# Attention times V in two blocks per chunk instead of four, in a fused attention and gated MLP kernel

## The chip, the cores and the metric

The kernel runs on one core of one Trainium2 chip. The metric is the device time of one execution in microseconds (us); lower is better. Three runs of the kernel before took 557.98, 558.04 and 558.1 us, median 558.04.

## The reference

One layer norm feeds a sliding-window attention and a gated MLP; both results are added to the input.

```python
xn = _layernorm(x)                                # S = 2048 rows, D = 576
qkv = (xn @ wqkv)                                 # H = 32 heads of Dh = 18
scores = q @ k.T * Dh ** -0.5                     # key at most 255 rows back, none ahead
o = softmax(masked scores) @ v
A = o @ wo
B = (silu(xn @ w1) * (xn @ w3)) @ w2              # F = 4608
return x + A + B
```

Inputs and output are bfloat16.

## The kernel before, in words

**Recording.** The kernel is written as one list of operations in program order. A helper, `add`, gives each operation its engine, the buffers it reads (`r`), overwrites (`w`) or adds to (`j`), and derives the semaphore waits. Each engine then runs its own operations in that order: TensorE (PE), VectorE (DVE), ScalarE (ACT), GpSimd (POOL), and SyncE (SP), which only issues DMAs. ScalarE issues some DMAs too, in line with its computing. An operation that waits holds up everything behind it in its engine's queue.

**Chunks.** The 2048 rows are worked in four chunks of 512. In chunks 2 to 4 a chunk begins with the projections to q, k and v (`proj_part`, L490). Then come 36 *units*, then *phase 2*. In chunk 1 the projections are done ahead of the loop.

**Units.** A unit makes 128 of the 4608 hidden columns: 18 products of 64 rows by 128 columns by 512 (`unit_pairs`, L726), two at a time on the two halves of the array, nine into each of two PSUM banks. ScalarE computes a tanh of one bank (`unit_tanh`, L735), VectorE multiplies twice (`unit_h`, L741 and L744) and writes the hidden tile `hT[u]`. Six of the eight PSUM banks are three pairs, `JOBS`, which units and V blocks take in turn (`job()`); the other two, `SC`, are for the scores.

**Attention.** The 32 heads are 8 groups of four. A *score step* (`scores`, L610) makes a part of the scores of one group; ScalarE writes its exponentials into a slot (`exps`, L619), GpSimd masks them (`masks`, L646). There are 4 steps per group in chunk 1 and 5 in the others, 32 and 40 steps per chunk, dealt out between the products of the units by a hand-written clock that counts pairs of products. Slots for probabilities lie in a buffer of their own (`pt`, 10 slots), in the staging buffer of the projections (`sh`, 4 slots, chunks 2 to 4) and in tiles of `hT` that aren't computed yet (`h`, 4 slots in the last 8 tiles).

**V blocks.** When two groups (a pair) are done, `pv` (L667) multiplies their probabilities with V: 72 products in chunk 1 and 96 in the others, 64 rows by 20 columns, eight side by side, into one pair of banks. A column of ones in V gives the sums of the probabilities. Then VectorE copies each of the two banks out in transposed form (`pv_out`, L676), takes the reciprocal of the sums (L681), GpSimd scales (`o_scale`, L682) into one buffer `oq`, and VectorE turns the result back in two halves (`o_turn`, L689) into `od`. DMAs pack it into `oT` (`o_pack`, L714): four packs per pair, and eight small ones for the first pair, which ScalarE issues in chunk 1 and SP in the others. Three V blocks stand between units, the fourth after item 8 of phase 2.

**Phase 2.** `p2_item` (L797) multiplies `hT` with w2 and `oT` with wo, in products of 64 by 128 by 288, two at a time, and adds both into the same banks. Some 324 items; the first two read a part of `oT` that only the first pair fills; the other products with wo of the first half follow after 144 items with w2. VectorE adds the input and SP stores.

**Weights.** The weights of the units pass through three buffers `w13`, each for four units, in six loads of 192 KB on SP (`load_part`, L320). `owed` counts loads to be issued, one after every fifth product pair. Buffer 1 holds tiles of w2 during phase 2. In chunks 2 to 4 the loads for the next chunk's first four units are issued after the 28th unit, those for its second four units in phase 2. w2 is loaded in tiles of 288 KB, six tiles ahead (`load_w2`, L352), on ScalarE's queue during phase 2.

**What the change touches:** the slots (`pt_slot`, `pt_keys`), the two staging places for copies out (`uqs`), `exps`, `pv`, `o_scale`, and in the main loop `PV_COST`, `take`, `score_step`, the V block after a unit, the block in phase 2, and the weight loads after units and in phase 2.

Of the kernel before, what the change touches and what calls it, by code (L numbers as in the profile page):

```python
# [164 lines left out]
def bass_parallel_sum__sliding_block__glu_gated_swiglu__prompt_kernel(  # L165
# [32 lines left out]
    with ExitStack() as es:  # L198
# [5 lines left out]
        KB, NB, NV = 64, CH // 64, 12  # L204
        ident = sb("ident", [128, 128])
# [27 lines left out]
        def pt_slot(sl):  # L233
            kind, n = sl
            if kind == "pt":
                return pt[:, n, :, :]
            if kind == "sh":
                two = stage[:, 2 * n:2 * n + 2, :]
            else:
                two = hT[:, NF - 8 + 2 * n:NF - 6 + 2 * n, :]  # L240
            return two.rearrange("p t c -> p (t c)").rearrange("p (q r) -> p q r", r=2)

        def pt_keys(sl):
            kind, n = sl
            if kind == "pt":
                return [("pt", n)]
            if kind == "sh":
                return [("sh", 2 * n), ("sh", 2 * n + 1)]
            return [("h", NF - 8 + 2 * n), ("h", NF - 7 + 2 * n)]
# [5 lines left out]
        rden = sb("rden", [128, CH // 32], dt.float32)  # L255
# [292 lines left out]
        def span_issue(a, b, moves, first, only=slice(None)):  # L548
            seen = set()
            for n, (kind, eng, tset, dst, src) in enumerate(moves):  # L550
# [4 lines left out]
                add(eng, lambda e, dst=dst, src=src: e.dma_start(dst, src), r=st_keys(*tset), dma=f"{kind}_{a}",  # L555
# [59 lines left out]

        def exps(c, g, s, sl):
            pt_of[(c, g, s)] = sl
            w = KB * sum(nb for _, _, nb in steps_of(c)[s])
            add("act", lambda e: e.activation(  # L619
                pt_slot(sl)[:, 0:w, :], PS[:, SC[0]:SC[1] + 1, 0:w].rearrange("p r q -> p q r"), ACT.Exp, scale=scale),  # L620
                r=[("ps", b) for b in SC], w=pt_keys(sl))
# [27 lines left out]
        def pv(c, j, banks):  # L649
# [4 lines left out]
            for s, st in enumerate(steps_of(c)):  # L654
                col = 0
                for kb, q0, nb in st:
                    n += 1
                    pos = (c * NB + kb) % NV
                    for gi in range(2):
                        g = 2 * j + gi  # L660
                        sl = pt_of[(c, g, s)]
                        for pr in range(2):
                            for p in range(2):
# [8 lines left out]
                                    r=pt_keys(sl) + [("va", pos)], **{"j" if any(k[0] == p for k in seen - {(p, gi, pr)}) or not first else "w": [("ps", banks[p])]})  # L672
                    col += nb

        def pv_out(b, i):
            add("dve", lambda e: e.transpose(uqs[i], PS[:, b, :]), r=[("ps", b)], w=uq_keys[i])  # L676

        def o_scale(i):
            u3 = uqs[i].rearrange("p (n d) -> p n d", d=32)
            o3 = oq[:, :].rearrange("p (n d) -> p n d", d=32)[:, :, 0:Dh]  # L680
            add("dve", lambda e: e.reciprocal(rden[:], u3[:, :, Dh]), r=uq_keys[i], w=["rden"])  # L681
            add("pool", lambda e: e.tensor_tensor(  # L682
                o3, u3[:, :, 0:Dh], rden[:].unsqueeze(2).to_broadcast([128, CH // 32, Dh]), ALU.mult),
                r=uq_keys[i] + ["rden", "oq0"], w=["oq"])
# [306 lines left out]
        PV_COST, PV_AFTER = 6.6, 20  # L991
# [6 lines left out]
        for c in range(NC):  # L998
# [8 lines left out]
            total = 9 * NF + len(att) + 3 * PV_COST  # L1007
# [9 lines left out]
            if c:  # L1017
                free += [("sh", n) for n in range(4)]
            early = [("h", n) for n in range(4)]
# [7 lines left out]
            def take(n):  # L1027
                if n < len(early):
                    return early[n]
                return free.pop(0)  # L1030

            def score_step():
# [3 lines left out]
                sl = take(done)  # L1036
                exps(c, g, s, sl)
                masks(c, g, s)
                done += 1
                if done % (2 * NS) == 0:  # L1040
                    pv_ready[done // (2 * NS) - 1] = clock + PV_AFTER

            def spaced_step():
# [3 lines left out]
                room = last - clock - PV_COST * (3 - next_pv) - 5 * sum(v > at_u for v in xt)  # L1047
# [21 lines left out]
            for u in range(NF):  # L1069
# [16 lines left out]
                if u % 4 == 3 and u < NF - 8 and (c or u != 15):  # L1086
                    owed += 6
                if next_pv in pv_ready and clock >= pv_ready[next_pv] and next_pv < 3:
                    j = next_pv
                    next_pv += 1  # L1090
                    banks = job()
                    pv(c, j, banks)
                    clock += PV_COST
                    for g in (2 * j, 2 * j + 1):
                        for s in range(NS):
                            if pt_of[(c, g, s)][0] != "h":
                                free.append(pt_of[(c, g, s)])
                    later(u, lambda b=banks: (pv_out(b[0], 0), pv_out(b[1], 1), o_scale(0)))
                    later(u + 1, lambda j=j: (o_turn(2 * j, 0), o_turn(2 * j, 1), o_scale(1)))
                    later(u + 2, lambda j=j: o_turn(2 * j + 1, 0))  # L1100
                    later(u + 3, lambda j=j: o_turn(2 * j + 1, 1))
                    later(u + 5, lambda j=j: o_pack(j, "sp"))
                    if j == 0:
                        for n in range(4, 12, 1 if c == 0 else 2):
                            later(u + n + 1 if c == 0 else u + n // 2 + 4,
                                  lambda n=n: o_pack(0, "act", n, n + 1) if c == 0 else o_pack(0, "sp", n, n + 2))
# [33 lines left out]
            assert done == len(att) and next_pv == 3, (done, next_pv)  # L1140
# [9 lines left out]
            for item in p2_list(c):  # L1150
# [8 lines left out]
                elif n == 8:  # L1159
                    load_w2(c, AHEAD - 1, after=(last_pe(),))  # L1160
                    banks = jobs[NF - 2]
                    pv(c, 3, banks)
                    pv_out(banks[0], 0)
                    pv_out(banks[1], 1)
                    o_scale(0)
                    o_turn(6, 0)
                    o_turn(6, 1)
                    o_scale(1)
                    o_turn(7, 0)
                    o_turn(7, 1)  # L1170
                    o_pack(3, "sp")
# [7 lines left out]
                elif n in (170, 195, 220, 245, 270, 295) and c + 1 < NC:  # L1179
# [32 lines left out]
```

## Time and profile before

| | |
|---|---|
| median of three runs | 558.04 us |
| lowest and highest | 557.98 and 558.1 us |
| the profiled execution's span | 556.1 us |
| TensorE busy, granted clock | 99% of the span, full |
| products of units (L726), share of the chain that ended last | 51% |
| products of phase 2 (L797) | 29% |
| projections (L490) | 10% |
| scores (L610) | 6% |
| V blocks (L667) | 4% |
| VectorE, ScalarE, GpSimd busy | 56%, 46%, 29% |
| moved by DMA | 86 MB, mean 155 GB/s |

The profile is of one execution. The span runs from its first instruction to its last; the runs are timed around it and are 1.9 us longer. In a row of the timeline the first number is the start in us from the span's beginning, the second how long the row lasts, then the engine, the line, the operation, output and inputs, the shape and how many instructions were merged. In brackets stands how long the engine was idle before, and what ended it. Matmuls are pipelined: one lasts longer in a row than the time to the next one's start, so the distance of starts tells what a product costs.

### The profile page before, as it was taken

Reading aid. Unit: us, or ns where it says so; the run is one execution under the profiler, and the core shown is the slowest. Engines: PE = TensorE matmul, PEld = TensorE weight load, DVE = VectorE, ACT = ScalarE, POOL = GpSimd, SP = SyncE. Lnnn points to the kernel's source line nnn. Section 1 sums busy time; section 2 is a strip of 40 time slices with the busy share of each in tenths; the row PEclk is TensorE's granted clock in tenths of the full one; section 3 lists DMA queues with packets and bytes.
Section 4 is the critical chain, followed back from the end, with each engine's and each line's share of the span. In section 5 each row is a group of like instructions: output and inputs, shape, how many; then the busy total and the mean of one; then the engine's idle time right before and its main releaser. Section 6 shows DMA issues by size and latency. Waiting matters only on the chain.

```text
span 556.1 us, 18239 instructions
## 1 busy us (share of the span) xinstructions
PE 552.4 (99%) x8022; PEld 348.8 (63%) x8022; DVE 310.8 (56%) x587; ACT 257.6 (46%) x365; POOL 160.0 (29%) x380
## 2 busy tenths in 40 slices
PE   8999999999999999999999999999999999999998
PEld 4555445677687455477767645547777654555776
DVE  7466798610456778851056668884105567767211
ACT  7456776100286767600047776650005676666000
POOL 5323454300034445330003344533000333433000
PEclk9999999999999999999999999999999999999999
DMA  9997899677566556656856746566683684650650
GB/s 255 203 197 161 201 215 182 171 179 191 139 139 149 135 147 151 155 148 176 205 109 137 171 110 170 126 163 164 158 205 83 138 174 124 151 135 21 174 152 22
DMA packets 128038, 86.00 MB, mean 155 GB/s; under 512 B 35702, under 2 KB 125646, under 8 KB 127958
## 3 DMA queue, kind: packets, MB, share of 16 engines
q1 hardware_dynamic: 89138, 62.80, 49.7%
q10 hardware_dynamic: 38820, 22.02, 16.0%
q8 instruction: 63, 1.03, 0.8%
q14 instruction: 17, 0.14, 0.1%
HBM read 71.29 MB, written 2.36 MB: 132 GB/s over the span
## 4 chain that ended last, share of the span: by engine, by line
PE 98%; DMA 1%; ACT 0%; DVE 0%; issue 0%
PE ps L726 51%; PE ps L797 29%; PE ps L490 10%; PE ps L610 6%; PE ps L667 4%; DMA xp<-in_A_x_dram 1%; DVE stats L386 0%; ACT hT L380 0%; PE ps L419 0%; ACT sd L359 0%; ACT xnT L432 0%; DVE ofin L819 0%; DVE mv L389 0%
## 5 line engine op out<-in xcount | busy, mean ns | idle before, releaser
L726 PE MATMUL ps<-xnT,w 64*128 64x512 bf16 x1400 | 182.3, 376 | 0.0
L726 PE MATMUL ps<-xnS,w 64*128 64x512 bf16 x1120 | 155.3, 376 | 0.0
L797 PE MATMUL ps<-w,hT 64*128 64x288 bf16 x2292 | 143.9, 282 | 0.0
L741 DVE SCALAR_TENSOR_TENSOR gs<-th,ps 128x512 bf16<-128x512 bf16 x144 | 98.0, 681 | 80.1 <-ACT th L735 79.1
L619 ACT ACTIVATE pt<-ps 128x1024 bf16<-128x1024 f32 (+1 forms) x112 | 113.2, 1010 | 63.8 <-PE ps L610 62.5
L797 PEld LDWEIGHTS ps<-w,hT 64*128 64x128 bf16 x2292 | 112.0, 94 | 29.4 <-issue 0.4
L726 PEld LDWEIGHTS ps<-xnT,w 64*128 64x128 bf16 x1400 | 73.8, 94 | 55.0
L646 POOL TENSOR_TENSOR pt<-pt,mk 128x128 int32<-128x128 int32 (+1 forms) x199 | 80.3, 426 | 79.5 <-ACT pt L619 79.5
L744 DVE SCALAR_TENSOR_TENSOR hT<-gs,ps 128x512 bf16<-128x512 bf16 x144 | 98.9, 687 | 5.0
L735 ACT ACTIVATE th<-ps 128x512 bf16<-128x512 f32 x144 | 85.4, 593 | 22.2 <-PE ps L726 21.9
L726 PEld LDWEIGHTS ps<-xnS,w 64*128 64x128 bf16 x1120 | 60.1, 94 | 50.1
L503 ACT ACTIVATE stage<-ps 128x512 bf16<-128x512 f32 x16 | 9.6, 597 | 142.8 <-PE ps L490 140.5
L828 DVE TENSOR_TENSOR ofin<-ps,xp 128x288 bf16<-128x288 f32 x31 | 12.2, 451 | 110.3 <-PE ps L797 110.3
L646 POOL TENSOR_TENSOR hT<-hT,mk 128x128 int32<-128x128 int32 (+1 forms) x31 | 12.4, 420 | 170.5 <-ACT hT L619 170.5
L610 PE MATMUL ps<-qv,kv 64*128 64x320 bf16 (+4 forms) x528 | 53.8, 260 | 0.0
L610 PEld LDWEIGHTS ps<-qv,kv 64*128 64x128 bf16 x528 | 28.5, 94 | 24.7 <-issue 0.3
L490 PE MATMUL ps<-xnT,wp 64*128 64x512 bf16 (+1 forms) x360 | 39.0, 355 | 0.0
L619 ACT ACTIVATE stage<-ps 128x1024 bf16<-128x1024 f32 x24 | 24.6, 1024 | 12.6 <-PE ps L610 12.6
L689 DVE STREAM_TRANSPOSE od<-oq 128x256 bf16<-128x256 bf16 x64 | 25.8, 428 | 6.3 <-POOL oq L682 6.3
L490 PEld LDWEIGHTS ps<-xnT,wp 64*128 64x128 bf16 x360 | 20.6, 94 | 12.6 <-ACT va L539 0.4
L490 PE MATMUL ps<-wv,xnT 64*128 64x288 bf16 x288 | 22.1, 284 | 0.2 <-ACT xnT L432 0.2
L646 POOL TENSOR_TENSOR stage<-stage,mk 128x128 int32<-128x128 int32 (+1 forms) x42 | 16.9, 421 | 17.4 <-ACT stage L619 17.3
(73 smaller groups left out, 337.6 us busy)
## 6 DMA issues: line engine op xcount, KB each, us to landing
w<-in_B_w_dram SPq DMA_DIRECT2D x210, 192.0 KB, 4.3
w<-in_B_w_dram ACTq DMA_DIRECT2D x70, 288.0 KB, 3.5
xp<-in_A_x_dram SPq DMA_DIRECT2D x29, 144.0 KB, 3.3
out_dram<-ofin SPq DMA_DIRECT2D x31, 72.0 KB, 3.2
xnS<-xnT SPq DMA_DIRECT2D x8, 256.0 KB, 5.2
oT<-od SPq DMA_DIRECT2D x56, 36.0 KB
pt<-in_A_wqkv_dram SPq DMA_DIRECT2D x4, 288.0 KB, 5.0
hT<-in_B_w_dram SPq DMA_DIRECT2D x6, 192.0 KB, 6.3
```

Source lines behind the costliest of these rows:

```text
L490: op = add("pe", lambda e, out_=out_, st=st, mv=mv, n=n, r0=r0, first=first: e.matmul(out_, st, mv, start=first, stop=(part == 1 and n == ...
L610: add("pe", lambda e, r0=r0, out_=out_, kb=kb, q0=q0, nb=nb: e.matmul(out_, kb4[r0:r0 + 64, g, kb + NV - NB, :] if kb < 0 else kv[r0:r0 + ...
L619: add("act", lambda e: e.activation(pt_slot(sl)[:, 0:w, :], PS[:, SC[0]:SC[1] + 1, 0:w].rearrange("p r q -> p q r"), ACT.Exp, scale=scale) ...
L646: add("pool", lambda e, vb=vb, mm=mm: e.tensor_tensor(vb, vb, mm, ALU.mult), r=(key if n == 0 else []) + ["mk"], **{"w" if n == 0 else "j" ...
L667: add("pe", lambda e, p=p, q=q, pr=pr, sl=sl, g=g, pos=pos, q0=q0, nb=nb, col=col, first=first, n=n: e.matmul(PS[32 * q:32 * q + VW, banks ...
L689: add("dve", lambda e: e.transpose(od[i][:, g % 2, c0:c0 + CH // 2], oq[:, c0:c0 + CH // 2]), r=["oq", "oq0"], **{"j" if half or g % 2 els ...
L726: op = add("pe", lambda e, n=n, r0=r0, r=r, k=k, src=src: e.matmul(PS[:, b0 + r, :], wt[r0:r0 + 64, k, fl * 128:(fl + 1) * 128], src, star ...
L735: add("act", lambda e: e.activation(th[i][:], PS[:, bg, :], ACT.Tanh, scale=0.5), r=[("ps", bg)], w=[("th", i)])
L741: add("dve", lambda e: e.scalar_tensor_tensor(out=gs[i][:], in0=th[i][:], scalar=1.0, in1=PS[:, bg, :], op0=ALU.add, op1=ALU.mult), r=[("t ...
L744: add("dve", lambda e: e.scalar_tensor_tensor(out=hT[:, u, :], in0=gs[i][:], scalar=0.5, in1=PS[:, bu, :], op0=ALU.mult, op1=ALU.mult), r= ...
L797: op = add("pe", lambda e: e.matmul(PS[:, bank, 0:w], stat, move, start=new, stop=False, skip_group_check=True, **tile), r=keys, after=hel ...
L828: add("dve", lambda e: e.tensor_tensor(ofin[:, o, :], PS[:, bank, 0:HD], xp[xs[n]][:, d0:d0 + HD], ALU.add), r=[("ps", bank), ("xp", xs[n] ...
```

## The change

The four V blocks of a chunk become two, of two pairs each: the first between units, once the first four groups are done, the second in phase 2 after item 24 instead of 8. Each takes two pairs of banks. The four banks of a block are copied out in a row, into `uq`, `ofin` and two `pt` slots that the block has read (`borrow`); each has its own reciprocal buffer. Scaling and turning then follow unit by unit.

Probabilities of four groups are held until the first block, and those of the other four until phase 2. So there are more slots: 8 in `hT` instead of 4 in chunks 2 to 4 (the last 16 tiles), the staging buffer in chunk 1 too, and 8 in the weight buffers 2 and 0 (`wx`), used from units 28 and 32 on, when their weights have been used for the last time in the chunk. The weight loads after the 28th unit are left out, and phase 2 has 12 loads from item 90 on, every 18 items, instead of 6 from item 170 on, every 25. DMAs that add late keys count on a semaphore of their own (`kr_`).

```diff
-                two = hT[:, NF - 8 + 2 * n:NF - 6 + 2 * n, :]
+                two = hT[:, NF - 2 * NHP + 2 * n:NF - 2 * NHP + 2 + 2 * n, :]
...
+            if kind == "wx":
+                b, i = WX[n]
+                flat = w13[b][:, :, :].rearrange("p a b -> p (a b)")
+                return flat[:, 2 * CH * i:2 * CH * (i + 1)].rearrange("p (q r) -> p q r", r=2)
...
-        rden = sb("rden", [128, CH // 32], dt.float32)
+        rden = [sb(f"rden{i}", [128, CH // 32], dt.float32) for i in range(4)]
...
-                add(eng, lambda e, dst=dst, src=src: e.dma_start(dst, src), r=st_keys(*tset), dma=f"{kind}_{a}",
+                add(eng, lambda e, dst=dst, src=src: e.dma_start(dst, src), r=st_keys(*tset), dma=f"{kind}_{a}" if first else f"{kind}r_{a}",
...
+        def lent_keys(c, sl):
+            keys = pt_keys(sl)
+            if sl[0] != "wx":
+                return {"w": keys}
+            b = WX[sl[1]][0]
+            if (c, b) in lent_w13:
+                return {"w": keys, "j": [("w13", b)]}
+            lent_w13.add((c, b))
+            return {"w": keys + [("w13", b)]}
...
+        def borrow(slots):
+
+            for i, n in enumerate(slots):
+                uqs[2 + i:3 + i] = [pt[:, n, :, :].rearrange("p q r -> p (q r)").bitcast(dt.float32)]
+                uq_keys[2 + i:3 + i] = [[("pt", n)]]
...
+        def o_recip(i):
+            u3 = uqs[i].rearrange("p (n d) -> p n d", d=32)
+            add("dve", lambda e: e.reciprocal(rden[i][:], u3[:, :, Dh]), r=uq_keys[i], w=[("rden", i)])
...
-        PV_COST, PV_AFTER = 6.6, 20
+        PV_COST, PV_AFTER = 12.4, 18
...
-                if done % (2 * NS) == 0:
-                    pv_ready[done // (2 * NS) - 1] = clock + PV_AFTER
+                if done == 4 * NS:
+                    pv_ready[0] = clock + PV_AFTER
...
-                if u % 4 == 3 and u < NF - 8 and (c or u != 15):
+                if u % 4 == 3 and u < NF - 12 and (c or u != 15):
                     owed += 6
-                if next_pv in pv_ready and clock >= pv_ready[next_pv] and next_pv < 3:
-                    j = next_pv
+                if next_pv in pv_ready and clock >= pv_ready[next_pv]:
                     next_pv += 1
-                    banks = job()
-                    pv(c, j, banks)
+                    pairs = [job(), job()]
+                    for j in range(2):
+                        pv(c, j, pairs[j])
...
-                    later(u, lambda b=banks: (pv_out(b[0], 0), pv_out(b[1], 1), o_scale(0)))
-                    later(u + 1, lambda j=j: (o_turn(2 * j, 0), o_turn(2 * j, 1), o_scale(1)))
-                    later(u + 2, lambda j=j: o_turn(2 * j + 1, 0))
-                    later(u + 3, lambda j=j: o_turn(2 * j + 1, 1))
-                    later(u + 5, lambda j=j: o_pack(j, "sp"))
+                    def drain(pairs=pairs, lent=lent):
+                        borrow(lent)
+                        for i in range(4):
+                            pv_out(pairs[i // 2][i % 2], i)
+                            o_recip(i)
+                        o_scale(0)
+
+                    later(u, drain)
+                    for g in range(4):
+                        later(u + 1 + 2 * g, lambda g=g: o_turn(g, 0))
+                        later(u + 2 + 2 * g, lambda g=g: (o_turn(g, 1), g < 3 and o_scale(g + 1)))
+                    for j in range(2):
+                        later(u + 5 + 4 * j, lambda j=j: o_pack(j, "sp"))
+                    for n in range(4, 12, 1 if c == 0 else 2):
+                        later(u + n + 1 if c == 0 else u + n // 2 + 5,
+                              lambda n=n: o_pack(0, "act", n, n + 1) if c == 0 else o_pack(0, "sp", n, n + 2))
...
-                    banks = jobs[NF - 2]
-                    pv(c, 3, banks)
...
+                elif n == 24:
+                    pairs = (jobs[NF - 2], jobs[NF - 1])
+                    borrow([m for kind, m in (pt_of[(c, g, s)] for g in range(4, G) for s in range(NS)) if kind == "pt"][:2])
+                    for j in range(2):
+                        pv(c, 2 + j, pairs[j])
+                    for i in range(4):
+                        pv_out(pairs[i // 2][i % 2], i)
+                        o_recip(i)
+                    for g in range(4):
+                        o_scale(g)
+                        o_turn(4 + g, 0)
+                        o_turn(4 + g, 1)
+                        if g % 2:
+                            o_pack(2 + g // 2, "sp")
...
-                elif n in (170, 195, 220, 245, 270, 295) and c + 1 < NC:
+                elif n in range(90, 300, 18) and c + 1 < NC:
                     load_part((last_pe(),))
```

65 lines of the change are left out of this document (30 added, 35 removed).

## The prediction

> **What bounds the kernel now.** I read the page's busy times, its clock row and the chain of work that ended last, then the waits.
>
> ```profile
> span 556.1 us, 18239 instructions
> ...
> PE 552.4 (99%) x8022; PEld 348.8 (63%) x8022; DVE 310.8 (56%) x587; ACT 257.6 (46%) x365; POOL 160.0 (29%) x380
> ...
> PEclk9999999999999999999999999999999999999999
> ...
> PE 98%; DMA 1%; ACT 0%; DVE 0%; issue 0%
> ```
>
> TensorE works through the whole span at its full granted clock and carries 98% of the chain. So only two things move the time: less work or fewer gaps on TensorE, or a new wait in front of it. The median of the runs, 558.04, is 1.9 us above the span; that part lies outside the kernel's work and I keep it as it is. A difference of 0.2% (1.1 us) is about what a measurement of this kernel can tell from no change.
>
> The only waits of TensorE that recur after the start are those of its weight loads in front of the V blocks (L667):
>
> ```profile
> PEld ps L667 <- issue: 3.1, 9, 0.4
> PEld ps L667 <- DVE gs L741: 2.5, 6, 0.4
> ```
>
> Fifteen of the sixteen blocks show about 0.37 us there, whoever is named. That points to something that belongs to a block's edge. One block of chunk 2, on TensorE's timeline:
>
> ```profile
> 195.78 0.38 PE L726 MATMUL ps<-xnS,w 64*128 64x512 bf16 x2
> 196.00 0.38 PE L726 MATMUL ps<-xnT,w 64*128 64x512 bf16 x2
> 196.31 0.32 PE L667 MATMUL ps<-pt,va 64*20 64x320 bf16 x4
> ...
> 197.23 0.30 PE L667 MATMUL ps<-stage,va 64*20 64x256 bf16 x4
> ...
> 197.35 0.30 PE L667 MATMUL ps<-stage,va 64*20 64x256 bf16 x4
> ...
> 197.61 0.40 PE L610 MATMUL ps<-qv,kv 64*128 64x320 bf16 x6
> 197.84 0.38 PE L726 MATMUL ps<-xnT,w 64*128 64x512 bf16 x2
> ```
>
> Two unit products side by side take 0.22 (195.78 to 196.00). The pair before the block takes 0.31 until the block starts: 0.09 lost going in. Inside, equal groups follow each other by 0.12 (197.23 to 197.35). The last one holds the next work back for 0.26 (197.35 to 197.61): 0.14 lost coming out. A block's edges cost 0.23 us, and each block of chunks 2 to 4 lasts 1.30.
>
> **The change, part by part.** *Fewer blocks.* The products of V are the same in number and shape. In each chunk the three blocks between units and the one in phase 2 become one and one, each of two pairs back to back. Two pairs of edges vanish per chunk, eight in all: 8 x 0.23 = 1.84 us off TensorE's own time. The Trainium skill (TensorEngine Tiling (Array Packing), section Tiling Modes) says that changing the tiling mode, not merely the tile, drains the engine, and its page TensorE: Matmul & The Clock Gate, section Single matmul latency, puts the drain at about 175 ns. By that two drains a block would make 8 x 0.35 = 2.8 us, an estimate from that page; the rows above show less per edge, and the sum goes by the rows. The seam inside a joined block isn't in the trace. From below it costs nothing beyond the usual 0.12, from above a whole edge pair (then the gain is nothing); I take nothing, since neither tile shape nor engine state changes at it.
>
> *Banks.* A block now holds two of the three bank pairs at once, so the next unit must take the pair of the unit just finished; before, it took a third pair, free long ago. It therefore waits until that unit's two VectorE multiplies have read it. In chunk 1 the order of the built program puts the new block behind the 22nd unit, where a block stood before too:
>
> ```profile
> 68.58 1.05 PE L667 MATMUL ps<-pt,va 64*20 64x320 bf16 x72
> 69.56 0.37 PE L610 MATMUL ps<-qv,kv 64*128 64x320 bf16 x4
> 69.76 1.03 PE L726 MATMUL ps<-xnT,w 64*128 64x512 bf16 x8
> ...
> 71.48 0.36 PE L610 MATMUL ps<-qv,kv 64*128 64x320 bf16 x4
> ```
>
> ```profile
> 69.05 0.59 ACT L735 ACTIVATE th<-ps 128x512 bf16<-128x512 f32 x1
> ```
>
> ```profile
> 68.48 0.81 DVE L386 BATCH_NORM_STATS2 stats<-xp 128x6 f32<-128x288 bf16 x2
> ...
> 69.67 0.69 DVE L741 SCALAR_TENSOR_TENSOR gs<-th,ps 128x512 bf16<-128x512 bf16 x1
> 70.39 0.69 DVE L744 SCALAR_TENSOR_TENSOR hT<-gs,ps 128x512 bf16<-128x512 bf16 x1
> 71.00 0.71 DVE L676 STREAM_TRANSPOSE uq<-ps 128x512 f32<-128x512 f32 x1
> 71.63 0.67 DVE L676 STREAM_TRANSPOSE ofin<-ps 128x512 f32<-128x512 f32 x1
> 72.23 0.21 DVE L681 RECIPROCAL rden<-uq 128x16 f32<-128x16 f32 x1
> ```
>
> The multiplies end at 71.08, 2.50 us after the block's start: statistics of the next chunk's rows and a late gate function (69.64) hold them up. The joined block lasts 0.98 + 0.84 (the second without its coming-out), then a score step of 0.20: the unit is wanted at 2.02. It is about 0.5 us late. In chunks 2 and 4 the block also stands where one stood before:
>
> ```profile
> 197.53 0.69 DVE L741 SCALAR_TENSOR_TENSOR gs<-th,ps 128x512 bf16<-128x512 bf16 x1 [0.54 <-ACT th L735]
> ...
> 198.25 0.69 DVE L744 SCALAR_TENSOR_TENSOR hT<-gs,ps 128x512 bf16<-128x512 bf16 x1
> ```
>
> The multiplies end 2.63 after the block's start (198.94 less 196.31); the unit is wanted at 1.30 + 1.16 + 0.23 = 2.69. No wait, but with only 0.06 to spare. I take 0.5 once and nothing for the other three, with 0 and 4 x 0.5 as ends.
>
> *The output chain in chunk 1.* Behind the block VectorE copies four banks out in a row (0.63 each) with a reciprocal each (0.21), 3.4 us; one reciprocal per copy as before, only earlier. Then come turns, multiplies and norm work. ScalarE's queue holds eight small packs of 8 KB in chunk 1, the first behind the gate function five units after the block; it needs the fourth turn, and the next exponentials are queued behind it.
>
> ```profile
> 75.00:80.00 5.00, 5.00 (x58) 2.49 (x56) 4.93 (x13) 3.70 (x6) 2.21 (x5) 1.00 1.20 189
> ```
>
> ```profile
> 75.46 0.91 DVE L404 TENSOR_SCALAR xn<-xp,mv,rstd 128x512 bf16<-128x512 bf16 x2
> ```
>
> ```profile
> 76.43 0.59 ACTq L714 DMA_DIRECT2D oT<-od  x1
> ...
> 77.69 0.92 ACT L619 ACTIVATE pt<-ps 128x896 bf16<-128x896 f32 x1 [0.41 <-PE ps L610]
> ```
>
> VectorE is full in this stretch (4.93 of 5 us). From its start at 2.50: 3.4 for the copies, four units' multiplies at 1.41, four turns at 0.39 (from 0.77 for two, below), 0.9 for a norm, 1.1 for statistics: the fourth turn ends near 15.0. TensorE needs 2.14 a unit with its score step (sixteen products and the step are 69.56 to 71.48, two more products 0.22), so five units end near 13.2 and the gate function at 13.8. The pack waits 1.2 us. Of that ScalarE has 0.41 to spare before an exponential, and a score step comes only each 2.1 us against 1.02 for the exponential, so TensorE feels between 0 and 0.8. I take 0.2, nearer to zero, because both margins come first. The other chunks issue these packs from SP, where no exponential is queued.
>
> *Phase 2.* The second block stands sixteen items later than before and delivers two head-group pairs there instead of one, so twice as many copies, scalings and packs stand before the products of wo.
>
> ```profile
> 100.70 0.41 PE L797 MATMUL ps<-wo,oT 64*128 64x288 bf16 x4
> ...
> 102.14 1.07 PE L667 MATMUL ps<-pt,va 64*20 64x320 bf16 x72
> ...
> 119.69 2.12 PE L797 MATMUL ps<-wo,oT 64*128 64x288 bf16 x32
> ```
>
> ```profile
> 106.10 0.77 DVE L689 STREAM_TRANSPOSE od<-oq 128x256 bf16<-128x256 bf16 x2 [0.79 <-POOL oq L682]
> ...
> 107.79 0.77 DVE L689 STREAM_TRANSPOSE od<-oq 128x256 bf16<-128x256 bf16 x2 [0.79 <-POOL oq L682]
> ```
>
> ```profile
> 108.59 2.96 SPq L714 DMA_DIRECT2D oT<-od  x4
> ```
>
> New start 102.14 + 16 x 0.12 = 104.1. Copies begin at 105.2 and end at 108.6, the first two turns at 109.4, three more pairs of turns at 1.48 (107.79 less 106.10, without the 0.21 of the reciprocal) at 113.8. Four packs at 0.74 each: the last is issued near 116.1. The products that need it are due 8 items after 119.69 + 0.84, near 121.5: 5.4 us for landing. Pack landings aren't listed; other loads are:
>
> ```profile
> w<-in_B_w_dram ACTq DMA_DIRECT2D x70, 288.0 KB, 3.5
> ...
> hT<-in_B_w_dram SPq DMA_DIRECT2D x6, 192.0 KB, 6.3
> ```
>
> At 3.5 us it is hidden, at 6.3 it is 0.9 late. I take 0. The first product of phase 2 (100.70) reads the small packs of chunk 1; the last is now issued behind the gate function two units earlier (1.94 to 2.14 each), some 3.6 to 4.1 us ahead: nothing at a landing of 3.5, up to 2.7 at 6.3; I take 0, since these are the smallest transfers.
>
> *Weight parts.* Six loads a chunk, 1.18 MB, move from the end of the units into phase 2 of chunks 1 to 3, since their buffer holds probabilities till then. On SP they stand behind the packs, which wait for VectorE, and so do one transposing load and two loads of x. None is wanted before the next chunk's first unit, 13 us after phase 2. The shared DMA engines:
>
> ```profile
> 103.00:141.60 38.60, 38.60 (x645) 30.11 (x630) 5.81 (x16) 0.00 (x0) 2.59 (x6) 1.00 0.75 187
> 130.00:135.00 5.00, 5.00 (x86) 3.98 (x82) 0.00 (x0) 0.00 (x0) 0.00 (x0) 1.00 1.00 254
> ```
>
> 187 GB/s becomes 187 + 1180 KB / 38.6 us = 218, below 254. w2 tiles are asked for six tiles (11.8 us) ahead and land in 3.5. Cost 0; without that lead a late tile would stop TensorE at once.
>
> *Exponentials, masks, semaphores.* Same number and shapes; only their place changes. Those in the weight buffer overwrite weights whose products stand earlier in TensorE's own order than the scores they wait for, so nothing is added. The separate count for late key moves adds a wait to a dozen score steps whose moves landed before. 0.
>
> Sum: -1.84 + 0.5 + 0.2 = -1.1, so 558.04 becomes 556.9.
>
> **The rivals.** *No new wait is felt:* the 0.5 and the 0.2 shrink because block and exponentials fall otherwise against each other; for it, the spare 0.06 in chunks 2 and 4; against, the 2.50 of chunk 1. 558.04 - 1.84 = 556.2.
>
> *Copying out becomes the limit in every chunk:* each joined block makes the next unit wait as in chunk 1: 4 x 0.5 + 0.2 - 1.84 = +0.4, 558.4. For it, the 0.06; against, VectorE has no statistics at that place in the other chunks. The Trainium skill (TensorEngine Tiling (Array Packing), section Performance Considerations) says that tiling speeds TensorE but not the reading out of PSUM; the trace bears that out at one block of four.
>
> *Slower: the packs of phase 2 land too late.* It decides from a landing of 5.4 us; the gain is gone at 5.7 and the 0.2% bound is passed at 6.0, since four chunks lose alike. For it, 1.00 DMA share in the row from 130, 31 GB/s more, and 6.3 us for some loads; against, the lighter stretch just before wo. At 6.3: 4 x 0.9 - 1.1 = +2.5, 560.5.
>
> **How the numbers follow.** Forecast 0.62, on its own 556.3 to 557.6; as it straddles the bound of 556.9, 0.34 of it counts as faster and 0.28 as the same. No new wait 0.14 (faster). Copying out 0.08 (same). Late packs 0.16 (slower). Faster 0.48, same 0.36, slower 0.16. The range, 555.5 to 559.1, holds the forecast, the second rival and most of the first; it leaves out most of the slower case and a larger gain, below 0.2 together.
>
> **What would show it.** Eight blocks of L667 instead of sixteen, each with 0.31 before and 0.26 behind and no gap at the seam; two waits less per chunk on L667; one wait of about 0.5 of L726 on VectorE's L744 (its new line) in chunk 1 after the block, and a score step held there by ScalarE; phase 2 without a wait of L797. A wait on oT or w2 in phase 2, or a unit wait behind each block, would make it wrong.

## The result, and the profile after

The changed kernel takes 562.67 us (median of five runs, 561.69 to 563.41) against 558.04 (557.89 to 558.10). The ratio is 1.0083, with a 95% interval from 1.0072 to 1.0095. It is slower by 4.6 us, where 1.1 less was predicted; the range ended at 559.1.

The page of the changed kernel, the lines that answer to those shown of before:

```profile
span 560.9 us, 18266 instructions
...
PE 551.8 (98%) x8022; PEld 380.1 (68%) x8022; DVE 315.7 (56%) x587; ACT 258.5 (46%) x365; POOL 161.3 (29%) x380
...
PEclk9999999999999999999999999999999999999999
...
q8 instruction: 63, 1.03, 0.8%
...
PE 93%; DVE 3%; DMA 2%; issue 1%; ACT 1%; ACTq 0%
```

The span is 4.8 us longer, and TensorE is busy for 0.6 us less. So it does the same work and stands still longer. The waits (engine, line, releaser: us in total, times, longest) say before what:

```profile
PEld ps L826 <- issue: 4.3, 5, 1.6
...
PE ps L826 <- issue: 3.1, 4, 1.3
...
PEld ps L686 <- issue: 2.6, 8, 0.4
...
PE ps L755 <- issue: 1.0, 1, 1.0
...
PE ps L826 <- DMA w<-in_B_w_dram: 0.4, 1, 0.4
...
PE ps L755 <- DVE hT L773: 0.3, 1, 0.3
```

(L826 is the old L797, L755 the old L726, L686 the old L667, L770 and L773 the old L741 and L744, L617 the old L610, L638 the old L619, L743 the old L714.) The eight blocks have their eight edges. The one wait of a unit on VectorE is there, and no product waits for oT. But four waits of phase 2 and one of a unit have "issue" as their releaser: TensorE waited for nothing that the profile names. The timeline of TensorE around the joined block in phase 2 of chunk 1 shows one of them:

```profile
104.65 0.32 PE L686 MATMUL ps<-stage,va 64*20 64x320 bf16 x4
...
106.49 1.15 PE L826 MATMUL ps<-w,hT 64*128 64x288 bf16 x15
108.96 0.79 PE L826 MATMUL ps<-w,hT 64*128 64x288 bf16 x10 [1.32 <-issue]
```

The block ends, 15 products of the next work run, and then TensorE stands, in the middle of products that are all alike and had all that they read. Chunks 2 to 4 show the same about 2 us behind each block of phase 2, chunk 1 also behind the block between its units, chunk 4 as well. Numbering all of TensorE's recorded instructions from 0 in order of start (8022 weight loads, 8022 matmuls, 95 semaphore waits and 2 drains; the last two kinds have to be counted too), and taking the packets of the instruction queue (q8) from the trace, gives this for every gap over 0.4 us that no semaphore explains:

```
resumes at  number  mod 256  from the start before  q8 packet ended  resumed after it
 72.65 us    1729     193        1.33 us               71.06            1.59 us
108.96       2753     193        1.60                 107.52            1.44
247.05       6849     193        1.15                 245.54            1.50
384.60      10945     193        0.75                 383.17            1.44
480.37      13761     193        0.41                 478.97            1.40
523.10      15041     193        0.74                 521.66            1.44
```

All six resume at the same place of a 256-count. The 63 packets of q8 have 1.03 MB, 16.4 KB each, and TensorE has 16,141 recorded instructions, 63 x 256 and 13 more. That gives the *supply theory*: TensorE's instructions come in pieces of 256; the next piece is fetched at about the time one is entered (in the six rows the packet starts 1.0 to 1.9 us later), and is needed at the next boundary. Around the second row above, in a window from 106.5 to 107.6 us of the DMA view, the fetch itself is seen:

```profile
DMA packets 11, 0.02 MB, mean 19 GB/s; under 512 B 2, under 2 KB 10, under 8 KB 10
...
q8 instruction: 1, 0.02, 5.3%
```

From one boundary to the next the trace of before has 3.70 us at the shortest (472.53 to 476.23) and no gap. A joined block issues 384 instructions in 2.5 us, 288 in 1.85 in chunk 1; a unit 36 in 1.95; phase 2 uses 256 in 7.84. So a piece that lies mostly in a joined block is used up in about 2 us. The Trainium skill (Runtime: NRT & Kernel Launch, section Instruction fetch mechanics) describes blocks of 256 instructions whose successor is fetched while one is executed, and calls the cost of a crossing mostly hidden. The first part agrees with the six rows; the second holds for the kernel before, and not here, where a crossing cost up to 1.6 us.

The rivals to it: the *bank theory*, in which VectorE's copying out of four banks holds TensorE, and the *transfer theory*, in which w2, weight parts and packs collide.

### The profile page after: what moved, and what is told of

It reads as the page before. It is cut to its first block, busy times and chain, and to the rows that moved or that the text cites. A ratio compares the mean times of both kernels' runs of the same rounds, so it can differ in the third digit from the quotient of the medians.

```text
span 560.9 us, 18266 instructions
## 1 busy us (share of the span) xinstructions
PE 551.8 (98%) x8022; PEld 380.1 (68%) x8022; DVE 315.7 (56%) x587; ACT 258.5 (46%) x365; POOL 161.3 (29%) x380
## 3 DMA queue, kind: packets, MB, share of 16 engines
q8 instruction: 63, 1.03, 0.8%
## 4 chain that ended last, share of the span: by engine, by line
PE 93%; DVE 3%; DMA 2%; issue 1%; ACT 1%; ACTq 0%
PE ps L755 48%; PE ps L826 27%; PE ps L497 9%; PE ps L617 5%; PE ps L686 3%; DMA w<-in_B_w_dram 2%; DVE gs L770 1%; DVE hT L773 1%; DVE stats L393 1%; DMA xp<-in_A_x_dram 0%; DVE xn L411 0%; ACT pt L638 0%; DVE od L718 0%; ACT th L764 0%; DVE mv L396 0%
## 5 line engine op out<-in xcount | busy, mean ns | idle before, releaser
L755 PE MATMUL ps<-xnT,w 64*128 64x512 bf16 x1400 | 186.9, 376 | 0.3 <-DVE hT L773 0.3
L755 PE MATMUL ps<-xnS,w 64*128 64x512 bf16 x1120 | 160.1, 376 | 1.0 <-issue 1.0
L826 PE MATMUL ps<-w,hT 64*128 64x288 bf16 x2292 | 144.9, 282 | 3.5 <-issue 3.1
L770 DVE SCALAR_TENSOR_TENSOR gs<-th,ps 128x512 bf16<-128x512 bf16 x144 | 98.1, 681 | 84.1 <-ACT th L764 83.9
L826 PEld LDWEIGHTS ps<-w,hT 64*128 64x128 bf16 x2292 | 121.9, 94 | 24.0 <-issue 4.3
L755 PEld LDWEIGHTS ps<-xnT,w 64*128 64x128 bf16 x1400 | 84.1, 94 | 50.4 <-DVE hT L773 0.6
L773 DVE SCALAR_TENSOR_TENSOR hT<-gs,ps 128x512 bf16<-128x512 bf16 x144 | 98.9, 687 | 5.0
L638 ACT ACTIVATE pt<-ps 128x1024 bf16<-128x1024 f32 (+1 forms) x80 | 81.0, 1013 | 44.2 <-PE ps L617 42.6
L755 PEld LDWEIGHTS ps<-xnS,w 64*128 64x128 bf16 x1120 | 67.2, 94 | 41.8 <-issue 1.5
L665 POOL TENSOR_TENSOR pt<-pt,mk 128x128 int32<-128x128 int32 (+1 forms) x144 | 59.4, 432 | 66.9 <-ACT pt L638 66.9
L665 POOL TENSOR_TENSOR hT<-hT,mk 128x128 int32<-128x128 int32 (+1 forms) x52 | 20.8, 420 | 175.7 <-ACT hT L638 175.7
L617 PE MATMUL ps<-qv,kv 64*128 64x320 bf16 (+4 forms) x528 | 56.4, 260 | 0.3 <-issue 0.2
L617 PEld LDWEIGHTS ps<-qv,kv 64*128 64x128 bf16 x528 | 31.9, 94 | 22.2 <-ACT pt L638 0.6
L638 ACT ACTIVATE hT<-ps 128x1024 bf16<-128x1024 f32 (+1 forms) x28 | 28.4, 1015 | 10.0 <-PE ps L617 9.9
L497 PEld LDWEIGHTS ps<-xnT,wp 64*128 64x128 bf16 x360 | 20.7, 94 | 12.4 <-ACT va L546 0.4
L638 ACT ACTIVATE stage<-ps 128x1024 bf16<-128x1024 f32 (+1 forms) x24 | 24.1, 1006 | 9.3 <-PE ps L617 9.2
L638 ACT ACTIVATE w<-ps 128x1024 bf16<-128x1024 f32 (+1 forms) x20 | 20.3, 1013 | 10.3 <-PE ps L617 10.3
```

The lines of the kernel that those rows point to most:

```text
L497: op = add("pe", lambda e, out_=out_, st=st, mv=mv, n=n, r0=r0, first=first: e.matmul(out_, st, mv, start=first, stop=(part == 1 and n == ...
L617: add("pe", lambda e, r0=r0, out_=out_, kb=kb, q0=q0, nb=nb: e.matmul(out_, kb4[r0:r0 + 64, g, kb + NV - NB, :] if kb < 0 else kv[r0:r0 + ...
L638: add("act", lambda e: e.activation(pt_slot(sl)[:, 0:w, :], PS[:, SC[0]:SC[1] + 1, 0:w].rearrange("p r q -> p q r"), ACT.Exp, scale=scale) ...
L665: add("pool", lambda e, vb=vb, mm=mm: e.tensor_tensor(vb, vb, mm, ALU.mult), r=(key if n == 0 else []) + ["mk"], **{"w" if n == 0 else "j" ...
L755: op = add("pe", lambda e, n=n, r0=r0, r=r, k=k, src=src: e.matmul(PS[:, b0 + r, :], wt[r0:r0 + 64, k, fl * 128:(fl + 1) * 128], src, star ...
L770: add("dve", lambda e: e.scalar_tensor_tensor(out=gs[i][:], in0=th[i][:], scalar=1.0, in1=PS[:, bg, :], op0=ALU.add, op1=ALU.mult), r=[("t ...
```

## The experiments

**The same work, moved by 64 instructions** (runs a_shift64 and b_shift64). In the changed kernel and in the one before, four of nine products of TensorE's warm-up become 36 small ones: 32 products more, each with its weight load.

```diff
-        warm(4, [CH] * 9)
+        warm(4, [CH] * 5 + [64] * 36)
```

> The changed kernel with nothing but 32 more small products in TensorE's warm-up before the first input lands (64 more instructions, each product is a weight load and a matmul). Supply theory: TensorE's instructions arrive in pieces of 256, the next piece is asked for when a piece is entered, and it takes about 3.5 to 4.1 us until it can be used; a joined block uses 384 instructions in 2.5 us, so it can outrun the supply. Where the boundaries of the pieces fall against the blocks then decides the loss: moved by 64 instructions, a whole piece lies inside nearly every joined block, each of the eight blocks loses about 2 us instead of about 0.7, and the time is 572 to 576 us; every gap without a wait ends at a boundary, 64 instructions earlier in the program than before. Bank theory (the next unit waits for VectorE to clear the banks) and transfer theory (blocks collide with w2, weight parts or packs): the work behind the start is the same, the time stays at 562.7 +-0.5.

> The kernel before with the same 32 small products at the start. Supply theory: a single block uses 192 instructions in 1.3 us and a piece always holds slower work beside it; at this position the shortest pieces of the blocks in phase 2 last about 3.4 to 3.7 us, at the edge of what the supply needs: 0.4 to 2.2 us more than before, 558.4 to 560.2 us. Bank and transfer theories: no change, 558.0 +-0.3.

The changed kernel took 576.86 us (573.43 to 581.52, ratio to before 1.0317, interval 1.0282 to 1.0352): 14 us more for 32 products that do not delay the first unit (it starts at 20.83 us, and at 20.88 in the changed kernel). The kernel before took 558.01 (ratio 1.0000, 0.9992 to 1.0009). The first is 0.9 above the upper edge of what the supply theory gave; for the second it had 0.4 to 2.2 us too much, since the shortest pieces there, 3.37 us, were still in time. The chain of the shifted kernel from 67 to 73 us (start, length, what):

```profile
67.47 1.74 PE ps L686 x115
69.21 2.97 issue
72.18 0.56 PE ps L686 x7
```

The gap now lies inside the block, between products of the same block that need nothing new. 130 of the block's 144 products had started before it; all read what the first ones waited for, into the same banks. All eight gaps, 0.65 to 3.18 us and 16.8 together, end at number 193 of 256 again, which is 64 instructions earlier in the program.

Those gaps (16.8 against 6.0) come to 10.8 us more than the changed kernel's. Its shortest run, at a granted clock of 1.000, has a span of 571.7 us, just 10.8 above the 560.9; the gaps were counted in another execution, so that the two agree so closely is partly luck. The profiled execution is its longest, 579.8 us at a mean clock of 0.985, and the windows around the gap show the difference (PE busy, PEld, DVE, ACT, POOL, then granted clock, DMA share, GB/s):

```profile
70.00:72.00 2.00, 0.00 (x0) 0.00 (x0) 1.60 (x4) 0.00 (x0) 1.10 (x3) 0.94 1.02 184
72.00:74.00 2.00, 1.82 (x24) 0.80 (x26) 1.17 (x3) 0.73 (x1) 0.00 (x0) 0.50 0.43 125
74.00:76.00 2.00, 2.00 (x18) 0.77 (x16) 0.62 (x2) 0.18 (x1) 0.73 (x2) 0.70 0.05 16
```

In the trace TensorE's granted clock is 0.50 for 3.4 us from 71.8, and again behind four later gaps. A mean of 0.985 over the span is about 8 us of 580, the rest. The changed kernel, whose gaps are 1.60 at most, kept the full clock. The Trainium skill (TensorE: Matmul & The Clock Gate, section What's actually happening) has a clock of one half after an idle window of about 3.4 us; the 0.50 agrees, the idle time does not, which was 2.97 us here.

**Only the blocks of phase 2 apart** (a_split2). The first pair stays after item 24, the second follows after item 56.

```diff
-                elif n == 24:
-                    pairs = (jobs[NF - 2], jobs[NF - 1])
...
+                elif n in (24, 56):
+                    j = n // 32
+                    pair = (jobs[NF - 2], jobs[NF - 1])[j]
...
+                    pv(c, 2 + j, pair)
```

> The changed kernel, but in phase 2 the two pairs of the block stand apart: the first where the joined block stood, the second 32 items later (3.9 us). Phase 1 keeps its joined block. Supply theory: the gaps of 1.60, 1.03, 0.64 and 0.62 us behind the joined blocks of phase 2 go, four more pairs of block edges at 0.23 come back: -3.9 + 0.9 = -3.0, 559.7 us. Bank theory: banks are not shared in phase 2, the edges come back alone, 563.6 us. Transfer theory: the same transfers run at nearly the same times, the gaps stay near where they were in time, 563 us or more.

559.58 us (558.70 to 562.42; ratio 1.0039, 1.0023 to 1.0054), 0.1 from the supply theory's sum and 4 from the bank theory's. No product of phase 2 stands at a boundary any more, and none waits for w2. A gap of 0.42 at a boundary in chunk 4 stays; the longest waits that remain are those of chunk 1:

```profile
PEld ps L755 <- issue: 1.6, 1, 1.6
...
PE ps L755 <- issue: 1.1, 1, 1.1
...
PEld ps L755 <- DVE hT L773: 0.6, 1, 0.6
```

**The bank's wait and the small packs of chunk 1 taken away** (a_nobank). Statistics four units earlier, small packs from SP.

```diff
-            near = {0: (20, 22, 23), 1: (24, 26, 27), 2: (30, 32, 33), 3: (33, 35, 40)}
+            near = {0: (16, 22, 23), 1: (24, 26, 27), 2: (30, 32, 33), 3: (33, 35, 40)}
...
-                        later(u + n + 1 if c == 0 else u + n // 2 + 5,
-                              lambda n=n: o_pack(0, "act", n, n + 1) if c == 0 else o_pack(0, "sp", n, n + 2))
+                        later(u + n // 2 + 5, lambda n=n: o_pack(0, "sp", n, n + 2))
```

> The changed kernel with the statistics that stood on VectorE beside the block of chunk 1 done four units earlier, and the small packs of chunk 1 issued from SP as in the other chunks, so that ScalarE's queue holds none. Bank theory: the unit's wait of 0.48 and the held score step of 0.24 go, 562.0 us, and the gap of 1.13 behind it in chunk 1 goes too if VectorE caused it, 560.8 us. Supply theory: the piece needed at the 1.13 gap comes no sooner, so the 0.48 only moves into that gap (1.6 us there); only the 0.24 can go: 562.4 to 562.7 us.

562.46 us (561.74 to 567.37; ratio 1.0099, 1.0072 to 1.0127): inside the supply theory's narrow band, but so near the changed kernel that the time alone decides little. The trace says more:

```profile
72.24 0.39 PE L755 MATMUL ps<-xnS,w 64*128 64x512 bf16 x2 [0.82 <-issue]
```

The unit's wait and the score step's are gone, and the gap without a waiter stays, at number 193: VectorE did not cause it. Yet it did not grow as expected. It shrank from 1.33 to 1.19, since this fetch ended at 70.88 instead of 71.06 and the resumption followed 1.36 after it instead of 1.59. From the first unit to the first product with w2 chunk 1 took 79.94 us instead of 80.62, so the two waits were real and worth about 0.7 there. In this execution a w2 tile was then 0.8 us late in chunk 3 (0.4 in the changed kernel), which took most of it back.

**Everything apart, the rest of the change kept** (a_split_all). In phase 1 the second pair stands behind the next unit (behind the second next in chunk 1), phase 2 as above.

```diff
-                    pairs = [job(), job()]
-                    for j in range(2):
-                        pv(c, j, pairs[j])
+                    pairs = [job()] if apart else [job(), job()]
+                    pv(c, 0, pairs[0])
...
+                        second.append((u + (2 if c == 0 else 1), behind))
```

> The changed kernel with every joined block taken apart: in phase 1 the second pair stands one unit behind the first (two units in chunk 1), in phase 2 32 items behind it. All else of the change stays: probabilities held longer, also in weight buffers, weight parts loaded in phase 2, statistics and small packs where the change has them. Supply theory: no block holds more than 192 instructions, at the worst a piece lasts about 3.4 us in phase 1 (two blocks with one unit between): at most a few tenths lost there, 557.9 to 559.0 us. Against it stands that the rest of the change costs the 4.7 us (weight parts against w2, longer holding, packs): then it stays at 560 us or more. A bank that is waited for would also be gone here, so this run does not tell bank from supply; a_nobank did.

558.68 us (558.35 to 563.45; ratio 1.0018, 1.0003 to 1.0033). So four of the 4.6 us go with the joining, the late w2 tile among them: nothing waits for w2 here. Some 0.7 stay with the rest of the change, and about half of that is one boundary, which still has a gap of 0.34 us, in the second of two blocks with one unit between. What the rest is was not separated (longer holding, borrowed weight buffers, moved loads).

**Density of instructions alone** (b_dense and b_sparse). Into phase 2 of each chunk of the kernel before go extra products of the V blocks' tiling, on weights that lie in SBUF anyway, into free banks. Nobody reads them. One kernel has 256 products of 256 columns (below), the other 128 of 512.

```diff
+                elif n == 92:
+                    for m in range(256):
+                        p, q = m % 2, m // 2 % 4
+                        add("pe", lambda e, p=p, q=q, b=jobs[NF - 1][p]: e.matmul(
+                            PS[32 * q:32 * q + VW, b, 0:256], wo[64 * p:64 * p + 64, 1, 0:VW], wo[64 * p:64 * p + 64, 0, 0:256],
...
```

> The kernel before with 256 extra products once in phase 2 of each chunk, of the V products' tiling (64 rows x 20 columns of weights, 256 columns moved) on weights of wo that lie in SBUF from chunk 1 on, into banks that are free there; nobody reads the result, nothing is loaded for it and no engine but TensorE takes part. By the rate of the V blocks (96 products in 1.30 us) they last 3.5 us with 0.23 for the edges. Supply theory: they are 512 instructions in 3.5 us, 1.75 us a piece, so TensorE stands 1.8 to 2.8 us a chunk at boundaries of pieces: 4 x (3.7 + 1.8 to 2.8) on 558.0, 580 to 584 us. Bank and transfer theories: no copying out and no new transfer, 572.8 +-0.8 us.

> The same as b_dense with half as many products of twice the columns (128 products that move 512 columns): the same columns through TensorE, 256 instructions instead of 512. Supply theory: a piece lasts 3.5 us or more, little or nothing is lost: 572.5 to 573.8 us. The difference of b_dense and b_sparse is what the density of instructions alone costs, 7 to 11 us. Bank and transfer theories: the same as b_dense within 0.8 us.

586.56 us (586.00 to 587.45) and 574.14 (572.91 to 574.21): the same columns, 12.4 us apart, where 7 to 11 were expected. The many are 2.6 above the upper end of their band, the few 0.3 above theirs. TensorE's timeline in chunk 1, the many products first and then the few:

```profile
113.60 2.04 PE L1175 MATMUL ps<-wo 64*20 64x256 bf16 x136
118.25 3.33 PE L1175 MATMUL ps<-wo 64*20 64x256 bf16 x120 [2.61 <-issue]
121.51 0.66 PE L797 MATMUL ps<-w,hT 64*128 64x288 bf16 x6
```

```profile
113.60 3.64 PE L1175 MATMUL ps<-wo 64*20 64x512 bf16 x128
117.18 0.66 PE L797 MATMUL ps<-w,hT 64*128 64x288 bf16 x8
118.57 3.71 PE L797 MATMUL ps<-w,hT 64*128 64x288 bf16 x57 [0.73 <-issue]
```

Nothing here but TensorE's own instructions has changed; no other engine and no transfer of data takes part. The many stand 2.9 us in their middle in chunk 1, and 11.6 at boundaries over the four chunks; the granted clock, 0.994 over the span of 585.7, adds some 3.5. The few were expected free, and stood 1.0 and 0.6 in two chunks: 256 instructions in 3.6 us are at the limit. The instruction queue's row of both pages, the many first, also counts as the theory needs: 2048 added instructions are 8 pieces, 1024 are 4.

```profile
q8 instruction: 71, 1.16, 0.9%
```

```profile
q8 instruction: 67, 1.10, 0.9%
```

**The late w2 tile** (a_wact). The weight parts of phase 2 go to ScalarE's queue.

```diff
-                    load_part((last_pe(),))
+                    load_part((last_pe(),), eng="act")
```

> The changed kernel with the weight parts of phase 2 issued from ScalarE's queue instead of SP's. Reading to be tested: in the changed kernel SP stands behind the packs, so that four of these parts go out at once (394.84 in chunk 3), w2 tiles land in 9.5 us instead of 5.5 and TensorE waits 0.4 us once for one of them (1.1 in a_nobank). If that is the cause, the parts go out evenly, no product of phase 2 waits for w2, and the time falls by 0.4 to 0.6 to about 562.2 us; the gaps at boundaries of the instruction pieces stay, four of 0.6 to 1.6 in phase 2. If the wait comes from the added bytes alone, it stays whatever queue they are in.

564.60 us (563.58 to 571.09; ratio 1.0146, 1.0111 to 1.0181): a miss. TensorE waited for w2 in chunk 2 instead of chunk 3, twice and 0.7 us in all. In the DMA view of chunk 3 from 395 to 419 us, w2 tiles (288 KB; the last number is the median time to landing) in the kernel before, in the changed kernel, in this one and in the one with only the blocks of phase 2 apart, in this order:

```profile
w<-in_B_w_dram ACTq DMA_DIRECT2D x7, 288.0 KB, 5.5
```

```profile
w<-in_B_w_dram ACTq DMA_DIRECT2D x9, 288.0 KB, 9.5
```

```profile
w<-in_B_w_dram ACTq DMA_DIRECT2D x9, 288.0 KB, 5.6
```

```profile
w<-in_B_w_dram ACTq DMA_DIRECT2D x8, 288.0 KB, 5.7
```

Landing took 4 us longer in the changed kernel. The added bytes alone do not do it: the kernel with the blocks of phase 2 apart has the same moved parts, moved 5.62 MB in this window against 5.26, and its tiles landed in 5.7 us without a wait. Nor does the queue alone: from ScalarE's queue the tiles of chunk 3 were in time again (5.6), but those of chunk 2, from 258 to 282 us, landed in 9.7, against 8.1 in the changed kernel. Late tiles were seen only with joined blocks in phase 2; why is open.

**Joined only where it is cheap** (a_best and a_best2). As everything apart, but the blocks between the units of chunks 2 to 4 stay joined. In a_best the one of chunk 4 stands a unit earlier, to bring a boundary to its middle (the last two lines below); in a_best2 it stays.

```diff
+                    apart = c == 0
...
-                    pv_ready[0] = clock + PV_AFTER
+                    pv_ready[0] = clock + (PV_AFTER if c + 1 < NC else 9)
```

> As a_split_all, but the block between the units stays joined in chunks 2, 3 and 4, where a boundary of the pieces falls near its middle; in chunk 4 it stands one unit earlier than in the changed kernel so that it does so there as well (its piece was the one with a gap of 0.41). In chunk 1 and in phase 2 the pairs stay apart. Supply theory: a piece that ends in the middle of a joined block has 192 of its 256 instructions in the block at most half the time and lasts 3.7 us or more: no gap above 0.3 us; three pairs of edges at 0.23 are saved against the kernel before: 557.3 us (557.0 to 557.7). Bank theory: a joined block makes the next unit wait by 0.2 to 0.5 in each of the three chunks, 557.9 to 558.8 us.

> As a_best, but the block of chunk 4 stands where the changed kernel has it. In a_best the piece that a product inside that block needed was asked for 2.34 us late and TensorE stood 1.52 us; at its old place it stood 0.41. Supply theory: chunks 1 to 3 as in a_best (in each of chunks 2 and 3 about 0.25 less than the kernel before), chunk 4 0.2 more than the kernel before: 557.4 to 557.9 us, within 0.1% of the kernel before. Bank theory: the joined blocks of chunks 2 to 4 make the next unit wait, 558.5 us or more.

a_best: 558.65 us (557.36 to 563.14; ratio 1.0015, 1.0001 to 1.0029), a miss: the fetch that mattered started 2.34 us after its boundary, and TensorE stood inside the block of chunk 4.

```profile
471.56 0.78 PE L686 MATMUL ps<-pt,va 64*20 64x192 bf16 x44 [1.27 <-issue]
```

a_best2: 557.66 us (557.28 to 560.66; ratio 0.9999, 0.9990 to 1.0008), as expected. No gap of over 0.2 us at a boundary is left; this is as fast as the kernel before, and not shown to be faster.

## Why the prediction was wrong

**What moves the time.** "So only two things move the time: less work or fewer gaps on TensorE, or a new wait in front of it." This step failed. It took TensorE's full span as work that can be packed at will, and left out that the instructions themselves must arrive. The page of before had the row for it, 63 packets of an instruction queue, and the length of the pieces could be counted in its trace:

```profile
q8 instruction: 63, 1.03, 0.8%
```

What the runs showed in its place: TensorE stood at six boundaries between pieces of 256 instructions, 5.4 us together, for which the sum had no term.

**The seam.** "From below it costs nothing beyond the usual 0.12, from above a whole edge pair (then the gain is nothing); I take nothing, since neither tile shape nor engine state changes at it." The seam itself is free: the second pair follows the first without a gap. But the bound from above, 0.23, was far too low. What joining removed was the slower work between two blocks, the time in which the next piece could arrive. The gaps at boundaries, 6.0 us from start to start (5.4 beyond the usual distance), are the largest term of the result. No rival had it either.

**Fewer edges, -1.84.** Right in mechanism and size. From the first unit of chunk 2 to that of chunk 3 the kernel before takes 137.32 us (155.12 to 292.44) and a_best2, with one join, 137.10 (154.99 to 292.09); from chunk 3 to 4 it is 137.25 (to 429.69) and 137.03 (to 429.12). A join saves 0.22; 0.23 was predicted.

**Banks, +0.5 in chunk 1 and 0 in the others.** Right. VectorE's and TensorE's timelines of chunk 1:

```profile
69.26 0.69 DVE L773 SCALAR_TENSOR_TENSOR hT<-gs,ps 128x512 bf16<-128x512 bf16 x1
```

```profile
67.45 0.32 PE L686 MATMUL ps<-hT,va 64*20 64x320 bf16 x4
...
69.33 0.37 PE L617 MATMUL ps<-qv,kv 64*128 64x320 bf16 x4
70.00 1.04 PE L755 MATMUL ps<-xnT,w 64*128 64x512 bf16 x8 [0.31 <-DVE hT L773]
...
72.65 0.39 PE L755 MATMUL ps<-xnS,w 64*128 64x512 bf16 x2 [0.96 <-issue]
```

The multiplies end at 69.95, 2.50 after the block's start, as worked out, and the unit starts at once: 0.67 after the score step's start, where 0.2 is usual. In the other chunks no unit waits.

**Small packs on ScalarE, +0.2.** Right: ScalarE issues two of them around an exponential, and the score step is late by about 0.24.

```profile
83.08 0.72 ACTq L743 DMA_DIRECT2D oT<-od  x1
...
83.84 1.02 ACT L638 ACTIVATE pt<-ps 128x1024 bf16<-128x1024 f32 x1 [1.17 <-DVE gs L770]
...
84.92 0.39 PE L617 MATMUL ps<-qv,kv 64*128 64x320 bf16 x6
```

Both waits together came to about 0.7 when a_nobank took them away.

**Packs of phase 2, 0.** Right: no product waits for oT, so the rival with late packs fell. That it had said slower, and the kernel is slower, is luck: its wait did not occur.

**Weight parts, 0.** Too low, and a wait for w2 had been named as a sign of being wrong: a w2 tile is late by 0.4 us (0.7 and 0.8 in the kernels with the parts on ScalarE's queue and with the bank's wait taken away). The mean rate that was worked out, 218 GB/s, was not exceeded: it is 206 from 103 to 142 us. But the price of 3.5 us for a landing was the median over the whole kernel; in the window above it was 5.5 already before the change and 9.5 after it. The tile waited for at 414.19 was asked for at 404.05 and took 10.1 us.

**The sum in hindsight,** from the distances of starts beyond the usual: -1.8 for edges, +0.5, +0.2 and +0.5 for the three waits (unit, score step, w2), and +5.4 for instructions that weren't there make +4.8, as in the spans. The kernel with everything apart, which undoes only the joining, bears out the last and largest term.

## What to carry to other kernels

Where an engine is packed without gaps, count its instructions as well as its time: each of the 28 pieces of 256 that these kernels used in 3.2 us or less was followed by a standstill, of 0.6 to 3.2 us, at boundaries that lie at fixed counts; of those used in 3.3 to 4.1 us ten were, and most were not. Joining dense blocks therefore needs slower work around every boundary, and any edit ahead that changes the number of instructions, be it only a warm-up, moves the boundaries against the blocks. A gap that resumes in the middle of like instructions, with "issue" as its releaser, is to be counted in instructions before a wait is sought.

## What was not expected of the hardware

In all 38 gaps of over 0.33 us at boundaries, over these kernels, TensorE resumed 1.22 to 1.63 us after the fetch packet had ended. The packet took 0.9 to 1.7 us, and in all but one gap it started 0.9 to 2.4 us after TensorE had crossed the boundary before. That is 3.3 to 4.9 us from boundary to boundary. What sets the start is open: over all 63 boundaries of the changed kernel the packet started between 1.3 us before the crossing and 5.2 us after it, so entering a piece doesn't by itself set it. Among the gaps it was late in chunk 1, in a_best and in the added products of chunks 1 and 2, and no run varied it by itself.

A long gap can cost more than its length. In the profiled executions of the shifted kernel and of the one with the many products the granted clock was 0.50 for 3.4 us behind each of the seven gaps of 2.16 us or more. It stayed full behind the other 31 gaps, of 2.07 us and less, of all kernels. The shifted kernel's shortest run shows a mean of 1.000 with the same instructions; how long its gaps were is not on record, so whether the length alone decides is open.
